# The last 128 tokens of FFN2 in column groups of 384, 256 and 128, each stored at once over two DMA queues

## The chip, the cores and the metric

The program runs on one core of one Trainium2 chip. The metric is device time in microseconds (us) of one execution. Most executions of a kernel agree within 0.3%, about 1.2 us here. A profile of one execution gives a trace with times in nanoseconds. Engines are PE (TensorE), DVE (VectorE), ACT (ScalarE), POOL (GpSimd) and SP (SyncE); SPq and ACTq are the instruction streams of SyncE and ScalarE, which also issue DMA transfers.

I call **tail** the time from the end of the last matmul to the end of the span. No tensor work hides anything there.

## The reference

```python
# 8 batches, 12 heads, 448 tokens, head_dim 64
scores = q @ k.T / sqrt(64)
attn   = maximum(scores, 0) ** 2 / 448
x      = (attn @ v) as [3584 tokens, 768]
h      = x @ w_in                                   # [3584, 2048], FFN1
g      = maximum(h, 0) + alpha * minimum(h, 0)
out    = g @ w_out                                  # [3584, 768] float32, FFN2
```

## The kernel before

Attention and both FFN layers are interleaved so that TensorE always has matmuls. The last batch has no attention left to interleave; its FFN1 and the last four of the seven FFN2 blocks of the last two batches run one after the other at the end. FFN2 takes 128 tokens at a time (index `c`), in two halves of 384 output columns (`hf`):

```python
    def ffn2(sb, c, hf, half):
        ...                                          # PSUM tile [128, 384] when half == 0
        for ff in range(8 * half, 8 * half + 8):
            nc.tensor.matmul(ps, gT[sb][:, ff, bass.ts(c, 128)],
                             w_out_sb[:, ff, bass.ts(hf, 384)],
                             start=(ff == 0), stop=(ff == KF - 1))      # KF = 16
        ...
        nc.vector.tensor_copy(o[:, bass.ts(hf, 384)], ps)
        if hf == 1:                                  # both halves there: store whole rows
            for u in range(2):                       # two blocks of 64 tokens
                blk = 2 * c + u
                b, j = 2 * sb + blk // NJ, blk % NJ
                rows = out[b * S:(b + 1) * S].rearrange("(pp j) d -> j pp d", j=NJ)
                nc.sync.dma_start(out=rows[j], in_=o[64 * u:64 * u + 64])
...
    for _, fn in steps(B - 1, "in") + steps(B - 1, "out"):
        fn()
```

A store writes 64 rows. Whole rows have 768 columns of 4 bytes, 3072 bytes each, 192 KB for a store.

## Time and profile before

| | before |
|---|---|
| time, median of 3 runs | 405.86 us (405.38 to 406.36) |
| span of the profiled run | 403.4 us |
| end of FFN1, last batch | 377.64 us |
| end of the last matmul | 398.44 us |
| tail | 4.93 us |

The lines that carry the reading are in the prediction. What they come to: TensorE is busy for 97% of the span and without a break at the end up to 398.44 us, so of what the change touches only the tail can shrink. The trace also lists each DMA packet by queue, which gives the tail in five pieces without slicing. These are not lines of a view but times read from the packets and landings of the trace:

```
before: last matmul ends 398.44
  0.60  wait and copy of 384 columns           -> 399.04
  1.15  until the first byte of a store        -> 400.19
  1.73  bytes of two stores, 384 KB            -> 401.92
  0.34  until the last store has landed        -> 402.26
  1.11  closing: semaphores and drains         -> 403.37
```

### The profile page before, as it was taken

The page shows a single profiled execution, that of the slowest core. Times are in us where ns is not written, and L with a number is a line of the kernel's source. Part 1 is how long each engine was busy: PE and PEld are TensorE (multiplying, and loading weights), DVE is VectorE, ACT ScalarE, POOL GpSimd, SP SyncE. Part 2 cuts the span into 40 slices and gives each one's busy share as a digit, 9 for nine tenths or more (in the row PEclk, how much of TensorE's full clock was granted, in tenths as well). Part 3 has the DMA queues.
Part 4 walks back from the last instruction along what each step waited for, and adds up shares of the span by engine and source line. Part 5 has one row for each costly group of instructions (what it writes and reads, how often), then busy time and mean ns, then how long its engine had stood idle before and what let it go on. Part 6 is the DMA issues. An engine that isn't in the chain of part 4 may idle for free.

```text
span 403.4 us, 7848 instructions
## 1 busy us (share of the span) xinstructions
PE 390.4 (97%) x3201; PEld 196.0 (49%) x3201; DVE 241.8 (60%) x379; ACT 232.1 (58%) x330; POOL 76.1 (19%) x88
## 2 busy tenths in 40 slices
PE   7689999999999999999999999999999999999995
PEld 4334455444555445544555445544455444555562
DVE  3966766687464793488643975556834666525411
ACT  5866745787564885387643876557653577524200
POOL 6653000033033330035000350033300300000000
PEclk9999999999999999999999999999999999999999
DMA  6999996593278941586065862379054720130033
GB/s 143 196 209 204 204 249 205 121 283 78 65 197 240 288 87 45 160 248 183 0 118 178 225 186 46 85 223 312 4 79 105 205 46 2 41 78 2 1 80 78
DMA packets 64164, 55.44 MB, mean 137 GB/s; under 512 B 35696, under 2 KB 59776, under 8 KB 64128
## 3 DMA queue, kind: packets, MB, share of 16 engines
q1 hardware_dynamic: 53152, 44.98, 41.6%
q0 software_dynamic: 10976, 9.96, 15.5%
q8 instruction: 25, 0.41, 0.4%
q14 instruction: 11, 0.09, 0.1%
HBM read 45.62 MB, written 11.01 MB: 140 GB/s over the span
## 4 chain that ended last, share of the span: by engine, by line
PE 90%; DMA 8%; issue 0%; ACT 0%; DVE 0%; SPq 0%; POOL 0%; POOLq 0%
PE ops L244 37%; PE hps L228 35%; PE sc L159 10%; PE av L199 7%; DMA qe<-in_q_dram 3%; DMA w_in_sb<-in_moe_w_in_dram 2%; DMA vb<-in_v_dram 2%; DMA kraw<-in_k_dram 1%; PE tps L134 1%; ACT xT L214 0%; DVE osb L252 0%; ACT ke L335 0%; SPq L321 0%; POOL ke L103 0%; PE warm L317 0%
## 5 line engine op out<-in xcount | busy, mean ns | idle before, releaser
L170 ACT ACTIVATE rl<-sc 128x896 bf16<-128x896 f32 x156 | 136.2, 919 | 80.0 <-PE sc L159 76.7
L228 PE MATMUL hps<-xT,w_in_sb 128*128 128x448 bf16 x768 | 154.8, 353 | 1.3 <-ACT xT L208 0.5
L244 PE MATMUL ops<-w_out_sb,gT 128*128 128x384 bf16 x896 | 154.3, 327 | 0.0
L181 DVE TENSOR_TENSOR at<-rl 128x896 bf16<-128x896 bf16 x167 | 115.2, 702 | 55.2 <-ACT rl L170 51.0
L244 PEld LDWEIGHTS <-gT 128*128 128x128 bf16 x896 | 84.0, 98 | 67.0 <-issue 14.5
L228 PEld LDWEIGHTS <-w_in_sb 128*128 128x128 bf16 x768 | 71.3, 98 | 79.0 <-issue 18.2
L236 DVE SCALAR_TENSOR_TENSOR gT<-neg,beta_sb,hps 128x448 bf16<-128x448 f32 x128 | 84.8, 676 | 31.8 <-ACT neg L235 30.7
L235 ACT ACTIVATE neg<-hps 128x448 f32<-128x448 f32 x128 | 69.8, 549 | 46.0 <-PE hps L228 45.4
L252 DVE COPY osb<-ops 128x384 f32<-128x384 f32 x56 | 31.1, 555 | 58.4 <-PE ops L244 58.4
L109 POOL CAST kb<-kraw 128x896 bf16<-128x896 f32 x16 | 16.1, 1007 | 210.4 <-DMA vraw<-in_v_dram 121.8
L159 PE MATMUL sc<-qT,kT 64*64 64x448 bf16 x652 | 50.8, 364 | 3.7 <-ACT rl L170 1.6
L199 PE MATMUL av<-at,vb 64*64 64x448 bf16 x616 | 33.1, 350 | 0.0
L159 PEld LDWEIGHTS <-kT 64*64 64x64 bf16 x672 | 14.5, 104 | 37.2 <-issue 33.7
L214 ACT ACTIVATE xT<-av 128x896 bf16<-128x896 f32 x21 | 19.3, 917 | 11.3 <-PE av L199 11.3
L199 PEld LDWEIGHTS <-vb 64*64 64x64 bf16 x672 | 19.7, 107 | 11.5 <-issue 1.7
L109 POOL CAST qb<-qraw 128x896 bf16<-128x896 f32 x16 | 20.0, 1250 | 0.0
L109 POOL CAST vb<-vraw 128x896 bf16<-128x896 f32 x16 | 18.6, 1165 | 0.4 <-DMA vraw<-in_v_dram 0.3
L144 POOL DMA_DIRECT2D w_in_sb<-in_moe_w_in_dram x12 | 7.5, 636 | 4.7 <-DMA vb<-in_v_dram 1.8
L168 DVE TENSOR_SCALAR rl<-sc 128x896 bf16<-128x896 f32 x6 | 6.5, 1086 | 2.9 <-PE sc L159 2.9
L317 PE MATMUL warm<-warm_x,warm_w 128*128 128x256 bf16 x24 | 4.6, 359 | 1.1 <-DVE warm_x L311 1.1
L134 PE MATMUL tps<-ident,ke 128*64 128x128 bf16 x84 | 3.7, 222 | 1.2 <-ACT rl L165 0.6
L107 ACT COPY kT<-tps 128x896 bf16<-128x896 bf16 (+1 forms) x4 | 3.2, 798 | 2.8 <-PE tps L134 2.7
(46 smaller groups left out, 59.0 us busy)
## 6 DMA issues: line engine op xcount, KB each, us to landing
out_dram<-osb SPq DMA_DIRECT2D x56, 192.0 KB, 2.7
qraw<-in_q_dram SPq DMA_DIRECT2D x19, 448.0 KB, 4.1
kraw<-in_k_dram SPq DMA_DIRECT2D x19, 448.0 KB, 5.0
vraw<-in_v_dram SPq DMA_DIRECT2D x18, 448.0 KB, 5.7
w_out_sb<-in_moe_w_out_dram POOLq DMA_DIRECT2D x2, 1536.0 KB, 20.2
w_in_sb<-in_moe_w_in_dram POOLq DMA_DIRECT2D x8, 192.0 KB, 8.4
w_in_sb<-in_moe_w_in_dram POOLq DMA_DIRECT2D x4, 384.0 KB, 9.9
vb<-in_v_dram POOLq DMA_DIRECT2D x6, 224.0 KB, 9.8
```

The costliest lines, as they stand in the source:

```text
L109: eng.tensor_copy(o, i)
L134: nc.tensor.transpose(ps[64 * s:64 * s + 64, j], t[:, s, j], ident)
L159: nc.tensor.matmul(half[r][64 * c:64 * c + 64, :S], kT[n][64 * r:64 * r + 64, j, c, :], qT[n][64 * r:64 * r + 64, :, c, :], start=True, st ...
L170: nc.scalar.activation(rl, ps[:, :, :S], ACTF.Relu)
L181: nc.vector.tensor_tensor(a, rl, rl, ALU.mult)
L199: nc.tensor.matmul(half[r][64 * s:64 * s + 64, :S], vb[n][64 * r:64 * r + 64, s, j, :], a[64 * r:64 * r + 64, s], start=(j == 0), stop=(j ...
L214: nc.scalar.activation(xT[b][:, g], ps[:, :, :S], ACTF.Copy, scale=out_scale)
L228: nc.tensor.matmul(ps, w_in_sb[:, km // 2, km % 2, bass.ts(ff, 128)], xT[b][:, km // 2, km % 2, :], start=(km == 0), stop=(km == KM - 1))
L235: nc.scalar.activation(neg, ps, ACTF.Relu, scale=-1.0)
L236: nc.vector.scalar_tensor_tensor(gT[b // 2][:, ff, (b % 2) * S:(b % 2) * S + S], neg, beta_sb[:, ff:ff + 1], ps, ALU.mult, ALU.add)
L244: nc.tensor.matmul(ps, gT[sb][:, ff, bass.ts(c, 128)], w_out_sb[:, ff, bass.ts(hf, 384)], start=(ff == 0), stop=(ff == KF - 1))
L252: nc.vector.tensor_copy(o[:, bass.ts(hf, 384)], ps)
```

## The change

The intent is to leave as little as possible behind the last matmul: the last copy is of 128 columns only, the other 640 columns of these tokens are already on their way, and the two stores of a group go out on two queues, SyncE's and ScalarE's.

```diff
+    def ffn2_last(sb, c):
+        o = o_sb[(sb, c)] = o_pool.tile([128, d_model], F32, tag="o", name="osb")
+        lo = 0
+        for w in (384, 256, 128):
+            ps = mm_ps.tile([128, 384], F32, tag="mm", name="ops")[:, :w]
+            for ff in range(KF):
+                nc.tensor.matmul(ps, gT[sb][:, ff, bass.ts(c, 128)], w_out_sb[:, ff, lo:lo + w],
+                                 start=(ff == 0), stop=(ff == KF - 1))
+            nc.vector.tensor_copy(o[:, lo:lo + w], ps)
+            for u in range(2):
+                blk = 2 * c + u
+                b, j = 2 * sb + blk // NJ, blk % NJ
+                rows = out[b * S:(b + 1) * S].rearrange("(pp j) d -> j pp d", j=NJ)
+                (nc.sync, nc.scalar)[u].dma_start(out=rows[j][:, lo:lo + w], in_=o[64 * u:64 * u + 64, lo:lo + w])
+            lo += w
...
-    for _, fn in steps(B - 1, "in") + steps(B - 1, "out"):
+    for _, fn in steps(B - 1, "in") + steps(B - 1, "out")[:-4]:
         fn()
+    ffn2_last(B // 2 - 1, NJ - 1)
```

## The prediction

> **What bounds the kernel now.** I read the page's engine shares first, then the chain of work that ended last, and then only the end of the trace, because the change touches nothing else: by the instruction order of the two built kernels, every engine has the same instructions in the same order up to the last 128 tokens.
>
> ```profile
> PE 390.4 (97%) x3201; PEld 196.0 (49%) x3201; DVE 241.8 (60%) x379; ACT 232.1 (58%) x330; POOL 76.1 (19%) x88
> PE 90%; DMA 8%; issue 0%; ACT 0%; DVE 0%; SPq 0%; POOL 0%; POOLq 0%
> ```
>
> TensorE (PE) is busy for 97% of the span and is 90% of the chain. So the body is bound by matmuls, and there the change has nothing to take. What it can win lies behind the last matmul. The timeline of the last microseconds (start, length, engine, line, names) shows that tail:
>
> ```profile
> 396.81 1.63 PE L244 MATMUL ops<-w_out_sb,gT 128*128 128x384 bf16 x9
> 398.48 0.56 DVE L252 COPY osb<-ops 128x384 f32<-128x384 f32 x1 [2.04 <-PE ops L244]
> 399.06 1.11 SPq L258 DMA_DIRECT2D out_dram<-osb  x2
> ```
>
> The last matmul ends near 398.45 us, the copy of its 384 columns out of PSUM takes 0.56 us, then SyncE's queue issues two stores in 1.11 us, one after the other. The span ends at 403.4, so 403.4 - 398.45 = **4.95 us** have no matmul. The stretches after it (length, then busy time of PE, weight loads, DVE, ACT, POOL; then clock, DMA share, GB/s) show when the bytes go:
>
> ```profile
> 399.50:400.00 0.50, 0.00 (x0) 0.00 (x0) 0.00 (x0) 0.00 (x0) 0.00 (x0) 1.00 0.00 0
> 400.00:400.50 0.50, 0.00 (x0) 0.00 (x0) 0.00 (x0) 0.00 (x0) 0.00 (x0) 1.00 0.72 166
> 400.50:401.00 0.50, 0.00 (x0) 0.00 (x0) 0.00 (x0) 0.00 (x0) 0.00 (x0) 1.00 0.96 197
> 401.00:401.50 0.50, 0.00 (x0) 0.00 (x0) 0.00 (x0) 0.00 (x0) 0.00 (x0) 1.00 0.94 320
> 401.50:402.00 0.50, 0.00 (x0) 0.00 (x0) 0.00 (x0) 0.00 (x0) 0.00 (x0) 1.00 0.46 105
> 402.00:402.50 0.50, 0.00 (x0) 0.00 (x0) 0.00 (x0) 0.00 (x0) 0.00 (x0) 1.00 0.00 0
> ```
>
> In finer slices of 0.1 us the DMA engines start at about 400.15 and are done at about 401.75. Reading the tail by these: copy with its wait 0.6 us (to 399.05), issue until the first byte 1.1 us (to 400.15), bytes 1.6 us (to 401.75), and the last landing near 402.25 (second issue at 399.6 plus a landing time of 2.6 to 2.7), 0.5 us after the last byte. The rest, about 1.1 us to 403.4, holds the closing semaphores and drains of all engines; the change leaves it alone. One thing is easy to misread here: the second issue (about 0.55 us) is not a term beside the others. The DMA engines are 96% and 94% busy from 400.5 to 401.5, so they work on the first store while the second is issued; what is on the path is the **amount of bytes behind the last copy**, 2 x 192 KB.
>
> **What the Trainium skill says.** "DMA: Bandwidth & Descriptors", section "Issuing engines are not separate DMA queues": copies issued by several engines run on the same 16 DMA engines and interleave; a second issuer saves only sequencer time. That agrees with the reading above, but no store of the kernel before is issued from ScalarE, so this trace has not tried it. The same page, "Anatomy of one DMA", puts a fixed cost of about 2.0 us on a transfer (fitted on the GpSimd path), most of it waiting for the write to be confirmed. The trace here has 1.1 us ahead of the first byte and 0.5 us behind the last, about 1.6 us; I use the trace. "TensorE: Matmul & The Clock Gate", section "Back-to-back issue gap", gives N/2.4 + 2.5 ns for an isolated gap, but about 81 ns for each pair of weight load and matmul at N = 128, where the formula says 56. At 384 and 448 columns the trace fits the formula (worked out below); at 128 columns with full 128-column weights it has nothing. "VectorE: DVE Perf Modes", in its section on the TRN2 errata, gives 120 + N cycles at 0.96 GHz for a copy out of PSUM: 525 ns at 384, where the trace has 557.
>
> **Part 1: narrower column groups on PE (a cost).** Two groups of 384 become 384, 256 and 128, that is 48 pairs of load and matmul in place of 32, with the same total of columns. Pace now: the chain has 128 matmuls of this line in 20.81 us, 162.6 ns each; the 96 of 448 columns before them took 18.16 us, 189.2 ns each. The slope is 26.6 ns for 64 columns, so 256 columns should take 162.6 - 128 x 0.416 = 109.4 ns and 128 columns 56 ns if the weight loads still hide. Whether they do is the open term. A load lasts 98 ns in the table:
>
> ```profile
> L244 PE MATMUL ops<-w_out_sb,gT 128*128 128x384 bf16 x896 | 154.3, 327 | 0.0
> L244 PEld LDWEIGHTS <-gT 128*128 128x128 bf16 x896 | 84.0, 98 | 67.0 <-issue 14.5
> L252 DVE COPY osb<-ops 128x384 f32<-128x384 f32 x56 | 31.1, 555 | 58.4 <-PE ops L244 58.4
> ```
>
> That is a length from start to end, and loads may overlap each other, as matmuls of 327 ns do that start every 163. Evidence: one early batch of 14 transposes (64-column weights, 128 columns streamed) took 0.58 us with 219 ns for one alone, so (0.58 - 0.219)/13 = 28 ns from one load to the next, far below their 106 to 110 ns. I choose 65 ns, between 56 and the skill's 81, nearer the low end; 98 would be no overlap at all. The end of a group is its last start plus the length of one matmul: 326 ns at 384 columns, 219 at 128 columns (the same transposes). Before: 31 x 162.6 + 326 = 5.37 us. After: 16 x 162.6 + 16 x 109.4 + 15 x 65 + 219 = 2.60 + 1.75 + 0.98 + 0.22 = 5.55 us. Cost **+0.18 us** (+0.05 at 56 ns, +0.42 at 81, +0.67 at 98), all on the path.
>
> **Part 2: a smaller last copy (a gain).** DVE's copies go at one column per 0.96 GHz cycle on this trace: 448 columns out of PSUM 616 to 625 ns, 384 columns 557, 16 columns 165. So 128 columns should take 557 - 256/0.96 = 290 ns: **-0.27 us**. The other copies (about 557 and 424 ns) lie beside the next group's matmuls.
>
> **Part 3: less to store behind it (the main gain).** Only 2 x 32 KB follow the last copy, not 2 x 192 KB. At the 200 to 250 GB/s seen above 64 KB would take 0.3 us; the pieces shrink from 3072 to 512 bytes, so I allow 0.45 us (an estimate). Then first byte to last falls from 1.6 to 0.45 us: -1.15 us. With a single queue the second issue would now show, as the first store's bytes would be through before the second's arrive; with ScalarE as second issuer both start together. If starting two at once costs something, say 0.2 us, the part gives **-0.95 us**. ScalarE is free: it has no work after 377.7 us.
>
> The earlier stores must be out of the way. With tB the end of the 256-column group: its copy ends at tB + 0.44, its first byte goes at tB + 1.5, its 128 KB at 240 GB/s are through near tB + 2.1. The last group's first byte goes at tB + 1.04 + 0.31 + 1.1 = tB + 2.45. They just miss each other, with some 0.35 us to spare.
>
> **Sum:** +0.18 - 0.27 - 0.95 = **-1.04 us**, or 0.26% of 405.86: 404.8 us. Each part is on the path, as the tail is a single file of copy, issue, bytes and closing.
>
> **The rivals.** (a) *Weight loads become the bound at 128 columns.* For: 98 ns each, and the skill's 81. Against: the transposes' 28 ns. It would give back up to 0.5 us: 405.3. (b) *The fixed latency of a store dominates and small rows are slow.* For: 1.6 us of the 3.2 us between the end of the copy and the landing is not bytes, and 512-byte rows carry more overhead each. If 64 KB take 1.0 us, the gain shrinks to about 0.5 us: 405.3. (c) *ScalarE's issue is slower or the two issues share something*, so that the second store starts no earlier than SyncE would have begun it. For: the kernel before never issues from ScalarE, and the descriptors may be made one after the other. It would add up to 0.5 us: 405.3. (d) *All goes well*: loads hide fully and both stores start at once: the gain is 0.27 + 1.15 - 0.05 = about 1.4 us: 404.5. A new queue might also cost something outside the span at start or end, which the trace of before cannot tell.
>
> **Range and chances.** The runs before spread from 405.38 to 406.36, about as much as the expected gain. From -1.04 with rivals (a) to (c) on one side and (d) on the other, plus half the spread, I take 404.1 to 405.7. Even no tail at all (4.95 us, 1.2%) would not make 2%, so "within 2%" is nearly certain: 0.985; faster by more 0.008; slower by more 0.007, for something unseen in the new queue.
>
> **What would show it.** Right: the last matmul ends about 0.2 us later than before; 128-column matmuls start 56 to 70 ns apart; the last copy takes 0.29 us; the two last issues, one on SyncE and one on ScalarE, start together within 0.1 us of its end; the DMA engines work for about half a microsecond some 1.1 us later; last matmul to end of span falls from 4.95 to about 3.7 us. Wrong: starts 80 to 98 ns apart (rival a), a DMA stretch of 1 us or more at the end (b), ScalarE's store landing clearly later than SyncE's (c), or the span shorter and the time not, which would put a cost outside the span.

## The result, and the profile after

The changed kernel takes 404.90 us in the median of 6 runs (404.43 to 405.76), the kernel before 406.11 us in 6 runs (405.38 to 407.26). The ratio is 0.9969 with a 95% interval of 0.995 to 0.9988. Ratios are computed as the mean time of one kernel's fast runs over that of the other's of the same rounds, so they are not quite the ratio of the medians. In the classes of 2% this is "same"; inside them it is a small, real gain.

The page of the changed kernel, its shares and chain, and the line of the new queue:

```profile
PE 392.8 (97%) x3217; PEld 197.9 (49%) x3217; DVE 241.6 (60%) x380; ACT 232.1 (58%) x330; POOL 75.5 (19%) x88
q10 hardware_dynamic: 240, 0.20, 0.2%
PE 94%; DMA 2%; ACT 1%; DVE 1%; issue 1%; POOL 0%
```

The queue q10 is ScalarE's: 240 packets, 80 for each of three stores (64 rows and 16 small ones for the semaphore). The chain must not be read as a result. Its DMA share fell from 8% to 2%, 24 us of span, in a kernel that is a microsecond faster: the chain follows the loads at the start by another way. Nothing of it is the tail.

The timeline of the end (start, length, engine, line):

```profile
394.46 5.40 PE L267 MATMUL ops<-w_out_sb,gT 128*128 128x384 bf16 x48
397.84 2.84 SPq L274 DMA_DIRECT2D out_dram<-osb  x3
397.85 2.99 ACTq L274 DMA_DIRECT2D out_dram<-osb  x3
399.00 0.42 DVE L269 COPY osb<-ops 128x256 f32<-128x256 f32 x1 [1.19 <-PE ops L267]
399.90 0.29 DVE L269 COPY osb<-ops 128x128 f32<-128x128 f32 x1 [0.47 <-PE ops L267]
```

The last copy is 0.29 us. And the stretches of its end, with the same columns as before (the last two are DMA share and GB/s):

```profile
400.00:400.50 0.50, 0.00 (x0) 0.00 (x0) 0.19 (x1) 0.00 (x0) 0.00 (x0) 1.00 0.00 0
400.50:401.00 0.50, 0.00 (x0) 0.00 (x0) 0.00 (x0) 0.00 (x0) 0.00 (x0) 1.00 0.69 184
401.00:401.50 0.50, 0.00 (x0) 0.00 (x0) 0.00 (x0) 0.00 (x0) 0.00 (x0) 1.00 0.49 126
401.50:402.00 0.50, 0.00 (x0) 0.00 (x0) 0.00 (x0) 0.00 (x0) 0.00 (x0) 1.00 0.32 83
```

It looks as if the bytes still took about 1.4 us. But these are two pairs of stores: by queue and size of packet, the 256-column pair moves from 400.58 to 401.30, and the last pair from 401.34 to 401.92. The five pieces, from the packets and landings as before:

```
after: last matmul ends 399.86
  0.33  wait and copy of 128 columns           -> 400.19      before 0.60
  1.15  until the first byte of the last pair  -> 401.34      before 1.15
  0.58  bytes of two stores, 64 KB             -> 401.92      before 1.73
  0.34  until the last store has landed        -> 402.26      before 0.34
  1.09  closing                                -> 403.35      before 1.11
  3.49  tail                                                  before 4.93
```

The tail is 1.44 us shorter: 1.15 us by fewer bytes, 0.27 by the smaller copy, 0.02 in the closing. From the end of FFN1 to the last matmul the core takes 20.84 us in place of 20.80, so the narrow groups cost 0.04 us. Sum: **-1.40 us**.

**Why do the two profiled spans differ by 0.1 us only, 403.4 and 403.3?** Because the last matmul ends at 399.86 and not at 398.44, and 377.64 had already become 379.02 at the end of FFN1, long before the change begins. Two stretches near the start, first of the kernel before, then of the changed one (the number after the last bracket is the granted clock):

```profile
10.00:15.00 5.00, 3.66 (x66) 1.98 (x67) 5.00 (x11) 4.20 (x6) 3.17 (x6) 1.00 1.22 192
15.00:20.00 5.00, 3.10 (x63) 1.87 (x64) 4.83 (x11) 4.71 (x9) 3.05 (x5) 1.00 1.23 198
```

```profile
10.00:15.00 5.00, 2.84 (x38) 1.39 (x42) 4.81 (x10) 3.83 (x6) 3.22 (x6) 0.69 1.19 177
15.00:20.00 5.00, 5.00 (x76) 2.81 (x67) 3.23 (x6) 3.45 (x6) 3.13 (x5) 0.63 1.25 204
```

In the second execution TensorE was granted 0.69 and 0.63 of its clock in these two stretches, and by the end of FFN1 the program was 1.4 us late. Whether that belongs to the change was a question for the experiments. The lesson for reading is plain already: compare the stretch that was changed, not the two span numbers.

### The profile page after: what moved, and what is told of

Read it like the earlier page. It is cut to its first block, busy times and chain, and to the rows that moved or that the text cites. A ratio compares the mean times of both kernels' runs of the same rounds, so it can differ in the third digit from the quotient of the medians.

```text
span 403.3 us, 7890 instructions
## 1 busy us (share of the span) xinstructions
PE 392.8 (97%) x3217; PEld 197.9 (49%) x3217; DVE 241.6 (60%) x380; ACT 232.1 (58%) x330; POOL 75.5 (19%) x88
## 4 chain that ended last, share of the span: by engine, by line
PE 94%; DMA 2%; ACT 1%; DVE 1%; issue 1%; POOL 0%
PE hps L228 37%; PE ops L244 36%; PE sc L159 10%; PE av L199 7%; DMA qe<-in_q_dram 1%; PE ops L267 1%; PE tps L134 1%; DMA qraw<-in_q_dram 1%; PE avh L199 1%; ACT rl L170 0%; DVE at L181 0%; PE sch L159 0%; ACT xT L208 0%; ACT xT L214 0%; POOL ke L103 0%
## 5 line engine op out<-in xcount | busy, mean ns | idle before, releaser
L244 PE MATMUL ops<-w_out_sb,gT 128*128 128x384 bf16 x864 | 149.1, 327 | 0.0
L244 PEld LDWEIGHTS <-gT 128*128 128x128 bf16 x864 | 80.9, 98 | 65.0 <-issue 14.4
L252 DVE COPY osb<-ops 128x384 f32<-128x384 f32 x54 | 29.9, 555 | 54.5 <-PE ops L244 54.5
L109 POOL CAST qb<-qraw 128x896 bf16<-128x896 f32 x16 | 18.9, 1179 | 0.0
L267 PE MATMUL ops<-w_out_sb,gT 128*128 128x384 bf16 (+2 forms) x48 | 5.4, 272 | 0.0
L134 PE MATMUL tps<-ident,qe 128*64 128x128 bf16 x84 | 3.5, 222 | 1.6 <-DMA qe<-in_q_dram 1.6
```

Of the source, the lines that this page charges most:

```text
L109: eng.tensor_copy(o, i)
L244: nc.tensor.matmul(ps, gT[sb][:, ff, bass.ts(c, 128)], w_out_sb[:, ff, bass.ts(hf, 384)], start=(ff == 0), stop=(ff == KF - 1))
L267: nc.tensor.matmul(ps, gT[sb][:, ff, bass.ts(c, 128)], w_out_sb[:, ff, lo:lo + w], start=(ff == 0), stop=(ff == KF - 1))
```

## The experiments

Theory **bytes**: what counts is how few bytes follow the last copy; the second queue is worth little. Rival **issue**: two stores issued one after the other from one queue are on the path, and the second queue is the gain. A third question is whether the narrow groups cost TensorE time, a fourth whether the lower clock at the start is part of the change. This table holds what all traces show. The pieces are read as above; "total" runs from the end of FFN1 to the end of the span, so that the start of the program, with its clock, is left out.

| run | last groups, queues | copy | to first byte | bytes | landing | closing | tail | total |
|---|---|---|---|---|---|---|---|---|
| before | 384 384, stored at the end, one | 0.60 | 1.15 | 1.73 | 0.34 | 1.11 | 4.93 | 25.73 |
| e4_before_again | the same | 0.60 | 1.15 | 1.70 | 0.34 | 1.09 | 4.88 | 25.68 |
| e2_two_queues | the same, two queues | 0.60 | 1.15 | 1.70 | 0.35 | 1.14 | 4.93 | 25.73 |
| e3_groups_only | 384 256 128, stored at the end, one | 0.33 | 1.15 | 1.72 | 0.34 | 1.09 | 4.63 | 25.47 |
| e1_one_queue | 384 256 128, at once, one | 0.33 | 1.67 | 0.94 | 0.35 | 1.36 | 4.64 | 25.48 |
| e12_last_pair_sync | the same, last pair on a queue of its own | 0.33 | 1.36 | 0.94 | 0.35 | 1.36 | 4.33 | 25.17 |
| e5_two_halves | 384 384, at once, two | 0.60 | 1.15 | 0.89 | 0.35 | 1.02 | 4.00 | 24.81 |
| after | 384 256 128, at once, two | 0.33 | 1.15 | 0.58 | 0.34 | 1.09 | 3.49 | 24.33 |
| e13_after_again | the same | 0.33 | 1.15 | 0.59 | 0.34 | 1.08 | 3.49 | 24.33 |
| e6_last64 | 384 320 64, at once, two | 0.26 | 1.64 | 0.46 | 0.34 | 1.18 | 3.88 | 24.72 |
| e8_six128 | six of 128, at once, two | 0.33 | 1.20 | 0.57 | 0.35 | 0.98 | 3.44 | 24.39 |
| e10_wait_order | as after, other semaphores | 0.33 | 1.15 | 0.59 | 0.34 | 0.98 | 3.40 | 24.24 |
| e11_512_160_96 | 512 160 96, other semaphores | 0.29 | 1.18 | 0.57 | 0.35 | 0.98 | 3.37 | 24.21 |

The repeats of before and after show how far a tail can be trusted: 4.93 and 4.88, 3.49 and 3.49. That is 0.05 us, where the times of the kernel before alone range over 2 us. All experiments gave correct results.

### e2_two_queues: only the second queue

```diff
-                nc.sync.dma_start(out=rows[j], in_=o[64 * u:64 * u + 64])
+                eng = nc.scalar if u and (sb, c) == (B // 2 - 1, NJ - 1) else nc.sync
+                eng.dma_start(out=rows[j], in_=o[64 * u:64 * u + 64])
```

> The kernel before with one edit: the second of the two last stores (192 KB each, after two groups of 384 columns) is issued by ScalarE. Theory 'bytes': the DMA engines are busy with the first store while the second is issued, 384 KB still have to go, so the tail stays 4.7 to 4.95 us. Rival 'issue': the second store starts and lands 0.55 us earlier, tail about 4.4 us. Also: if the new queue by itself costs something at the start of the program (the profiled run of the changed kernel had a lower clock from 10 to 20 us and was 1.4 us late by then), this run shows a mean clock of 0.991 to 0.996 and the kernels with one queue show 1.0; if that is chance of the run, there is no such split.

Measured: 405.90 us in the median, ratio 1.0008 (0.999 to 1.0027), tail 4.93 us, no gain at all. The timeline of its end shows that the edit does what it says, ScalarE issuing right behind the copy, and the queue lines of that stretch show a store on each queue (packets, MB, share):

```profile
400.06 0.56 DVE L252 COPY osb<-ops 128x384 f32<-128x384 f32 x1 [2.04 <-PE ops L244]
400.65 0.55 ACTq L259 DMA_DIRECT2D out_dram<-osb  x1
q1 hardware_dynamic: 80, 0.20, 25.9%
q10 hardware_dynamic: 80, 0.20, 12.7%
```

By the packets, SyncE's store moves from 401.77 to 402.99 and ScalarE's from 402.79 to 403.46, though both were issued within 5 ns. The second store's bytes come after nearly all of the first's. 384 KB take 1.70 us, from two queues as from one. So with 192 KB stores the second issue is fully hidden, as the prediction said, and the rival "issue" is refuted here.

### e3_groups_only: only the narrow groups

The three groups are computed and copied as in the change, but the two stores of whole rows follow the last copy, both on SyncE:

```diff
-            for u in range(2):                       # inside the loop over groups
-                ...
-                (nc.sync, nc.scalar)[u].dma_start(out=rows[j][:, lo:lo + w], ...)
             lo += w
+        for u in range(2):
+            ...
+            nc.sync.dma_start(out=rows[j], in_=o[64 * u:64 * u + 64])
```

> Column groups 384, 256, 128, but the whole rows stored after the last copy by two stores on SyncE's queue, as before. Measures the matmul and copy part alone. Expected: the 48 matmuls take 5.25 us instead of 5.20 (128-column matmuls 56 ns apart), the last copy 0.29 us, tail 4.95 - 0.27 = 4.7 us, in all about 0.2 us faster than before, under the noise of the times. If narrow groups cost, the matmuls take 5.4 us or more.

Measured: ratio 1.0008 (0.999 to 1.0025), as expected not to be told from before by time; FFN2 20.84 us for 20.80, tail 4.63 us. The tail loses 0.30 us, 0.27 by the small copy, and the rest is within the spread of the repeats. In total 0.26 us are gained.

### e1_one_queue: everything but the second queue

```diff
-                (nc.sync, nc.scalar)[u].dma_start(...)
+                nc.sync.dma_start(...)
```

> The change with all six last stores on SyncE's queue (column groups 384, 256, 128 kept). Read: the tail, from the end of the last matmul to the end of the span; 4.95 us in the kernel before, 3.43 us in the changed one. Theory 'bytes' (what counts is how few bytes follow the last copy; the second queue is worth nothing): tail stays 3.4 to 3.5 us. Rival 'issue' (two serial issues of some 0.5 us each are on the path once the bytes are few): the 256-column stores hold SyncE's queue until about 0.25 us after the last copy, then come two issues, so the last store lands about 0.5 us later and the tail is 3.9 to 4.0 us. I hold the second: with 64 KB the bytes no longer cover the second issue.

Measured: ratio 0.9998 (0.9982 to 1.0015), tail 4.64 us. That is 1.15 us worse than with two queues and no better than e3, which stores everything at the end. My expectation of 3.9 to 4.0 us was a miss: the sign was right, the size less than half. The timeline of its end shows SyncE issuing six stores in one row, from 397.90 for 4.00 us, until 1.65 us after the last copy is done at 400.24:

```profile
397.90 4.00 SPq L274 DMA_DIRECT2D out_dram<-osb  x6
399.06 0.42 DVE L269 COPY osb<-ops 128x256 f32<-128x256 f32 x1 [1.19 <-PE ops L267]
399.95 0.29 DVE L269 COPY osb<-ops 128x128 f32<-128x128 f32 x1 [0.47 <-PE ops L267]
```

Each store takes the queue about 0.5 to 0.6 us, so a pair needs 1.1 to 1.2, and the last group of matmuls takes only 0.9. The 256-column pair still holds the queue when the 128 columns are ready: the last pair is issued at 400.71, 0.47 us after the copy, and its second store at 401.31. By the pieces of the table the 1.15 us are these:

- **Queue still busy:** 0.44 us (the issue begins 0.47 us after the copy in place of 0.03), and 0.08 from that issue to the first byte (1.21 in place of 1.13). The 256-column bytes are not in the way: they are through at 401.71, and the last pair's first byte comes at 401.92.
- **Second store behind the first:** the bytes take 0.94 us in place of 0.58, 0.36 us.
- **Closing:** 1.36 us in place of 1.09, 0.27 us, by the order in which the program waits for its stores (e12 and e10 below). That part goes with the semaphore that the last store happens to have, not with the queue itself; a one-queue version with another order was not run.

### e12_last_pair_sync: which part of a single queue costs

```diff
-                (nc.sync, nc.scalar)[u].dma_start(...)
+                (nc.sync if w == 128 else nc.scalar).dma_start(...)
```

> The changed kernel, but the two stores of the 384- and of the 256-column group both on ScalarE's queue and the two last stores (128 columns) both on SyncE's. Takes the backlog of the 256-column stores out of the one-queue version (tail 4.64 us) and leaves the second serial issue. If one serial issue is the cost of a single queue: the second store starts its bytes 0.6 us after the first in place of 0.28, and its semaphore is the second in SyncE's closing order, so that seven waits follow its landing: tail 3.49 + 0.33 + 0.27 = 4.1 us. The rest to 4.64, about 0.5 us, is then the backlog of the stores ahead. If the backlog is nothing: 4.6 us. If the serial issue is nothing: 3.5 us.

Measured (one look): tail 4.33 us, between the 4.1 expected and the 4.6 of the rival. The queue of the last pair is free here, and its first store is issued at once:

```profile
397.17 2.74 ACTq L274 DMA_DIRECT2D out_dram<-osb  x4
399.22 0.29 DVE L269 COPY osb<-ops 128x128 f32<-128x128 f32 x1 [0.47 <-PE ops L267]
399.54 1.31 SPq L274 DMA_DIRECT2D out_dram<-osb  x2
```

- **Serial issue:** the second store's bytes start 0.64 us after the first's in place of 0.28, so the bytes take 0.94 us and not 0.58: 0.36 us.
- **Closing:** the store that lands last now has the second semaphore in SyncE's closing order, and seven more waits follow it: 1.36 us in place of 1.09, 0.27 us.
- **Later first byte:** it comes 1.36 us after the copy in place of 1.15: 0.21 us. This term I had not foreseen. ScalarE's 256-column store is still being issued when SyncE's issue begins, and its bytes still move until 401.02; which of the two holds the first byte back was not tested.

Together 0.84 us, the difference of the tails (4.33 - 3.49). The first two terms are those of e1 (0.36 and 0.27). The third is this run's own, since in e1 the 256-column bytes were through, so the 0.31 us up to e1's 4.64 are not the whole price of a busy queue: e1's own trace gives 0.44.

So the two parts of the change need each other. Alone, the second queue gains 0.00 us (e2) and early storing with narrow groups 0.24 us of total (e1, 25.726 - 25.482); together they gain 1.40. Without e1's closing term of 0.27 us the 0.24 would be about 0.5, an estimate from these numbers.

### e5_two_halves: two queues and early storing, groups of 384

```diff
-        for w in (384, 256, 128):
+        for w in (384, 384):
```

> The changed kernel with column groups 384 and 384 in place of 384, 256 and 128: each stored at once over both queues. Theory: the two parts of the change (fewer bytes behind the last copy, two queues) need each other, and the tail is copy + 1.155 us to the first byte + bytes + 0.34 us to landing + closing. With 2 x 96 KB the bytes should take 0.88 us (the 384-column pair of the changed kernel), the copy 0.56: tail 0.56 + 0.03 + 1.155 + 0.88 + 0.34 + 1.0 = 3.95 to 4.05 us. Rival 'it is the second queue and early storing, the width of the last group matters little': tail about 3.5 us as in the changed kernel.

Measured: 404.87 us, ratio 0.9972 (0.9948 to 0.9996), tail 4.00 us, within the 3.95 to 4.05 expected. The sum copy + first byte + bytes + landing + closing forecasts a tail from the width of the last group. Of the change's 1.40 us, 0.92 (25.73 - 24.81) come with two groups stored at once over two queues; the third group adds 0.48.

### e6_last64: a narrower last group

```diff
-        for w in (384, 256, 128):
+        for w in (384, 320, 64):
```

> Column groups 384, 320 and 64. Measures (1) whether the weight loads become the bound below 128 columns: if loads hide, 64-column matmuls start 29 ns apart and the last group takes 0.5 us; if a load needs 53 ns or more, 0.9 us or more. (2) How close the stores stand: the 320-column pair should end its bytes near 2.4 us after that group's last matmul, so the last pair's bytes, ready at 1.9 to 2.3 us, would queue behind them; the gain of the smaller last copy (0.225 us in place of 0.29) is lost. From the end of FFN1 to the end of the span: 24.3 us in the changed kernel; here 24.3 to 24.6 expected, so no gain.

Measured (one look): total 24.72 us, worse than the changed kernel and a little worse than expected. FFN2 takes 20.84 us all the same, so even 64-column matmuls are not held up by weight loads. Here are groups by shape from the end of its trace (count, busy time, mean length of one in ns):

```profile
L267 PEld LDWEIGHTS <-gT 128*128 128x128 bf16 x47 | 3.6, 98 | 1.7
L267 PE MATMUL ops<-w_out_sb,gT 128*128 128x64 bf16 x16 | 0.6, 193 | 0.0
```

Sixteen matmuls of 64 columns are busy for 0.6 us in all, though each has a weight load of 98 ns before it. Their starts are 29 ns apart in the trace. A load's length is not its pace. The loss is in the stores: the copy is 0.07 us shorter, but SyncE's queue is still issuing its 320-column store, and the last pair's issue begins 0.39 us after its copy ended; the first byte comes after 1.64 us in place of 1.15.

### e8_six128: six groups of 128

```diff
-        for w in (384, 256, 128):
+        for w in (128,) * 6:
```

> Six column groups of 128. Matmuls: 96 at 56 ns in place of 5.24 us, so 5.4 us (+0.16). Each group takes 0.9 us and its two stores 0.5 to 0.62 us of each queue, so the queues keep up: last copy 0.29, first byte 1.155 us after it, bytes 0.58. If stores that come every 0.9 us pile up (each pair's bytes take 0.58), the last pair starts later and the tail grows over 3.5 us. Expected tail 3.35 to 3.5 us, FFN1's end to the end of the span 24.4 us: no better than the changed kernel.

Measured (one look): total 24.39 us, tail 3.44 us, as expected. Stores every 0.9 us on two queues do not pile up; the extra matmuls cost 0.16 us (20.96 for 20.80). Its last stores happen to have late places in the closing order (0.98 us), so the fair measure for its total is e10, 24.24 us.

### e10_wait_order: the closing

```diff
-    nc.sync.dma_start(out=alpha_sb, in_=moe_alpha.rearrange("(kf p) -> kf p", p=128))
...
     load_bf16(1, "v")
+    nc.gpsimd.dma_start(out=alpha_sb, in_=moe_alpha.rearrange("(kf p) -> kf p", p=128))
```

The stores use eight semaphores in turn, and SyncE closes the program with one wait for each, always in the same order. In the trace of the changed kernel these waits start at 402.01, 402.07, 402.14, 402.20, 402.26, 402.32, 402.38 and 402.44: 62 ns apart. The first of them follows the landing of SyncE's last store at 401.99; the others are for stores that have landed by the time of their wait. Which semaphore the last store has thus matters.

> The changed kernel with one load (8 KB of alpha, early in the program) issued by GpSimd, not SyncE. This shifts by one which semaphores the last stores get. In the changed kernel SyncE closes with waits on the store semaphores in a fixed order, some 62 ns each; one of the last two stores has the second semaphore of that order, so seven waits (0.43 us) come after its landing at 401.99 and end at 402.47, though the very last landing is 402.26. Here the last two stores have the last two semaphores, so only one wait follows the last landing. Theory 'wait order is on the path': tail 3.49 - 0.17 = 3.3 us. Rival 'the closing is a fixed 1.1 us after the last landing': tail 3.5 us. In time 0.17 us is under the noise.

Measured: 404.17 us (403.53 to 404.44), ratio 0.9952 (0.9923 to 0.998), tail 3.40 us. From the last landing to the drain after the waits it is 0.14 us in place of 0.24. So the order is on the path, but for 0.09 to 0.10 us and not 0.17: I had counted the whole row of waits from the earlier landing and forgotten that a last wait and a drain are left in any case.

### e4_before_again and e13_after_again: the noise, and the clock

> The kernel before, unchanged, as a control. Expected: ratio 1.000 within 0.002, tail 4.95 us within 0.05, and a mean clock in its runs as in the other runs of this job (0.99 to 1.0). If its clock is 1.0 in all runs while the kernels with a second queue have 0.991 to 0.996, the dip at the start belongs to the change.

> The changed kernel, unchanged, in five rounds beside the kernel before on this chip, for the size of the whole effect. The tails say -1.40 us (ratio 0.9965). Expected ratio 0.995 to 0.998. If the mean clock of its runs has the same spread (0.990 to 1.000) as that of the kernel before, the clock dip near the start in its first profile was chance and not part of the change.

The control gave a ratio of 1.0014 (0.9998 to 1.003). The repeat of the changed kernel, in another job (chip 4) and with five rounds, gave 404.31 us beside 405.57, ratio 0.9958 (0.9941 to 0.9975), -1.7 us with an interval of 1.0 to 2.4. Both estimates of the whole effect include the 1.40 us of the tails. The clock is settled by the traces. The kernel before, profiled again in e4, has the dip too (the same two stretches):

```profile
10.00:15.00 5.00, 3.46 (x54) 1.81 (x53) 5.00 (x10) 4.20 (x7) 4.28 (x7) 0.87 1.21 187
15.00:20.00 5.00, 4.36 (x68) 2.38 (x60) 4.08 (x8) 4.26 (x8) 2.31 (x5) 0.79 1.22 190
```

e1, with one queue, has 0.58 and 0.74, while e5, e10 and e11, with two queues, have 1.00 in both. So the dip is a chance of the run and not a part of the change. What it costs is less clear. In e13's job the runs of the kernel before at a mean clock of 0.990 took 406.56 to 407.14 us and those at 0.998 took 404.91 to 405.57. But in e4's job its runs at 1.0 took 405.52 to 406.00, while e1's run at 0.991 took 405.09; and in the traces FFN1 ends at 377.64 to 378.43 us without a dip and at 378.14 to 379.27 with one. A lower clock tends to go with a later program, but it is not the whole of the noise, and neither its cause nor its cost was tested.

### e11_512_160_96: a version meant to beat both

```diff
-        for w in (384, 256, 128):
-            ps = mm_ps.tile([128, 384], F32, tag="mm", name="ops")[:, :w]
+        for w in (512, 160, 96):
+            ps = mm_ps.tile([128, 512], F32, tag="mm", name="ops")[:, :w]
```

with the alpha load of e10.

> A version meant to beat both: column groups 512, 160 and 96, both queues, alpha loaded by GpSimd so that the last stores have the last semaphores of the closing order. Worked from the tails seen: 96-column matmuls 42 ns apart, last copy 0.257 us, the 160-column pair done before the last pair's first byte, 2 x 48 KB... 2 x 24 KB in about 0.5 us: from FFN1's end to the end of the span 24.15 us, against 24.24 with groups of 384, 256, 128 and the same closing, 24.33 in the changed kernel and 25.73 before. In time about 1.6 us faster than before, ratio 0.996; not to be told from the changed kernel by time. Rival: the narrower last group brings the stores too close (as with 384, 320, 64) and it is 24.4 or more.

Measured: 404.09 us (403.59 to 404.29, 6 runs), ratio to before 0.9953 (0.9938 to 0.9969). Its total is 24.21 us, 0.06 above the 24.15 expected and under the 24.4 of the rival, 0.03 us better than e10 and 0.12 us better than the changed kernel in the same part of the trace; 0.11 of the 0.12 is the closing. It beats the kernel before clearly. Against the changed kernel it is ahead by the trace only; the intervals of the times overlap. A larger gain from the width of the groups isn't in sight: of its tail of 3.37 us, 2.51 are first byte, landing and closing (1.18 + 0.35 + 0.98), and a narrower last group did not shorten these (e6: 1.64 + 0.34 + 1.18).

## Why the prediction was right

The time predicted was 404.8 us, the time measured 404.90. By its steps:

- **What bounds the kernel:** right. The change gains only in the tail, and FFN2 costs 0.04 us more. The start of the program differs from run to run, in the kernel before as well.
- **"The second issue is not a term beside the others":** right, and the least obvious step. e2 moves that issue to another queue and gains nothing. The reason given was misread, though. By the prediction's own lines the second issue is over at 400.17 (399.06 + 1.11), and the first byte moves only at 400.19, so it is not the DMA engines' work that covers the issue but the 1.15 us before the first byte; and by the packets the second store's bytes begin at 401.11, before the first's end at 401.27.
- **"With a single queue the second issue would now show":** right, but undersized where I put numbers to it later. One queue costs 1.15 us (e1): 0.44 queue still busy, 0.08 more to the first byte, 0.36 second store behind the first and 0.27 closing. "The first store's bytes would be through before the second's arrive" holds: in e1 they end at 402.21, and the second's begin at 402.55. The prediction's other small misreading, that ScalarE has no work after 377.7 us (its last operation ends at 378.22), changed nothing.
- **Part 1, matmuls:** predicted +0.18 us at a chosen 65 ns, measured +0.04. The 128-column matmuls start 55 to 56 ns apart. I had that figure from the slope of 384 and 448 columns and moved away from it toward the skill's 81 ns. The transposes in the same trace were better evidence than I made of them: they start two at a time, a pair every 56 ns, so the 28 ns is a mean, and 128 columns of weights and 128 streamed columns go by in 56 ns. Rival (a) is refuted.
- **Part 2, copy:** predicted -0.27 us, measured 0.291 us for 0.558: right. (Of the lengths it was drawn from, those of 448 and 16 columns are VectorE operations with a scalar, not copies.)
- **Part 3, bytes:** predicted from 1.6 to 0.45 us, measured from 1.73 to 0.58. Both ends were 0.13 us too low, so the difference of 1.15 us is exact. The 0.2 us that I took off for "starting two at once" was not to be taken off on top: the 0.58 us already hold the 0.28 us by which the second store starts later. That left -0.95 where -1.15 was true.
- **"They just miss each other, with some 0.35 us to spare":** right in sign, but the spare time was 0.04 us (401.30 to 401.34). The 256-column pair took 0.71 us for its bytes, not the 0.55 of 128 KB at 240 GB/s, and the faster matmuls brought the last pair 0.14 us earlier (16 x 9 ns). Standing a little closer did no harm yet: in e11 the pair before moves until 0.15 us after the last pair's first byte, which comes after 1.18 us. In e6 it is mostly the late issue that costs (0.36 of 0.48 us).
- **Rival (b)**, slow small rows: partly so. 64 KB in 512-byte pieces took 0.58 us, 113 GB/s, against 227 GB/s for 384 KB in 3072-byte pieces. It was far from the 1.0 us of that rival. Whether it is the length of the pieces or the size of the whole transfer was not separated.
- **Rival (c)**, the two issues share something: the bytes of two stores issued together go one after the other (0.28 us apart for 32 KB, 1.03 us for 192 KB). By the sign that the prediction set it came in part true, as ScalarE's last store lands 0.27 us after SyncE's (402.26 and 401.99). Whether the order comes from making the transfers or from moving them is open, and so is what it costs: the DMA share is only 0.49 and 0.32 from 401.0 to 402.0 us.
- **"Tail falls from 4.95 to about 3.7 us":** 3.49. The sum of the steps was -1.04 us; the traces show -1.40, and the times, by the ratios, -1.3 (first rounds) and -1.7 (repeat). The mechanism was right and the gain about a quarter too small, by the terms of parts 1 and 3. That the median agreed to 0.1 us was partly luck, as the kernel before had slower runs beside it (406.11) than in its first three (405.86).

## What to carry to other kernels

Behind the last matmul, write the tail down as a sum (copy, first byte, bytes, landing, closing) and shorten the bytes: store early, keep the last group small, and stop where the stores of the group before still hold the queue (e6). Splitting stores into smaller ones and giving them a second queue belong together: while transfers are large (192 KB here) a second queue gains nothing, and when they are small (96 to 32 KB here) a single queue ate all that storing early had gained. Where an effect is smaller than the spread of the times, measure the changed stretch in the trace, from one fixed event to the end, and repeat both kernels to see how far it can be trusted.

## What the Trainium skill lacked or had wrong

- "TensorE: Matmul & The Clock Gate", "Back-to-back issue gap": its sustained 81 ns per pair of weight load and matmul at 128 columns was not seen. Pairs ran 56 ns apart at 128 columns (96 of them in a row in e8), 43 at 96 and 29 at 64 (e11, e6), which is the same page's formula for an isolated gap, N/2.4 + 2.5 ns. Its 131 ns at 512 columns was not seen either: 216 ns in e11.
- "DMA: Bandwidth & Descriptors", "Issuing engines are not separate DMA queues": e2 agrees that a second issuer by itself brings the bytes no sooner. But the issue is not "usually small relative to the DMA itself" for small stores: a 32 KB store moved its bytes in 0.30 us and took the queue 0.5 to 0.6 us, and a single queue cost 1.15 us here, 0.27 of it by the closing order.
- The same page, "Anatomy of one DMA": the fixed 2.0 us is for the GpSimd path. For a store by SyncE or ScalarE the page has only a first byte after about 600 ns ("Latency and other measured facts") and does not say from where that counts. Here, for SyncE's last store, it was 1.13 us from the start of the issue and 0.66 us from its end; the landing came 0.35 us after the last byte.
- "VectorE: DVE Perf Modes", the section on the TRN2 errata: 120 + N cycles for a copy out of PSUM gives 258 ns at 128 columns; measured 291. The copies of 64, 96, 128, 256, 384 and 512 columns (225, 258, 291, 425, 558 and 692 ns) fit 152 + N cycles at 0.96 GHz.
- No page that I read has the closing waits: one for each of eight store semaphores, in a fixed order, 62 ns apart, so that the semaphore of the last store is worth up to 0.38 us (the closing takes 1.36 us in e12 and 0.98 in e10).
